# Moving operands of TensorE placed 64 bytes beyond their stationary ones, modulo 256 bytes, in a three-stage attention and MLP kernel

## Chip, cores, metric

The kernel runs on one core of a Trainium2 chip. The metric is the device time of one execution in microseconds (us); lower is better. TensorE (PE), VectorE (DVE), ScalarE (ACT), GpSimd (POOL) and SyncE (SP) each run their own instruction stream; weight loads of TensorE are shown apart as PEld.

## The reference

Batch 2, sequence 3136, model width 256. Three layers follow each other:

```python
scores = z @ z.T / 3136                       # d_qk = 64
x = u * (maximum(scores, 0)**2 @ v)           # attention, gated

h = x.T @ U @ V                               # rank 32, over the sequence
a = x + h.T
x = a + maximum(a @ w_ch1, 0) @ w_ch2         # layer 1, hidden width 1024

m = real(fft(fft(x, axis=1), axis=2))
a = x + m
un = (a - mean(a)) / sqrt(var(a) + 1e-6)
out = a + maximum(un @ w_ch1b, 0) @ w_ch2b    # layer 2
```

## The kernel before

All matrix products are in fp32r (fp32 data read by TensorE in one pass). To keep precision, each operand is split into a high and a low part, and each product is three matmuls: high x high, high x low, low x high. Nearly every matmul has a moving operand of 448 columns (`CH`).

**Attention** (`attention`, from L421). For each batch and each of 7 blocks of 448 queries there are 13 steps, one a pair of key blocks. `scores` (L574) writes a key block's scores to PSUM: K = 64 (the head width), so two matmuls share the array, one on partitions 0 to 63 and one on 64 to 127; stationary is `KT`, moving is `Q`. ACT and DVE turn the scores into `P`, `h` (high) and `l` (low). `products` (L616) multiplies them by the values, two steps later (`LAG`): stationary is `Vt`, moving are `h` and `l`, again 64 rows in each half of the array. A full step has 3 pairs of matmuls for scores and 12 for values, so 15 pairs; a block of 13 steps has 186 pairs, 3 of them only 224 columns wide.

**Layers 1 and 2** (`Chunk`, L246). A layer has 14 chunks of 448 tokens, and a chunk 8 steps. A step issues 12 full 128-row matmuls: six in `hidden` (L368, L369, L370, twice: stationary the first weight matrix, moving `h` and `l`), then six in `project` for an earlier step (L393, L394, L395, twice: stationary the second weight matrix, moving `Hh` and `Hl`, the split result of `hidden`). Between the steps stand a few matmuls of other work: low-rank sums (L234), the Fourier transform (L956 to L958, L995, L1013 to L1018), layer norm sums (L308, L327).

The order of the instructions is written out by hand (`tc.manual_schedule()`), and tiles come from pools in which they lie one behind the other, so a tile's byte address in a partition follows from the sizes of the tiles and pools declared before it. The pools in question are `const` (masks, Fourier tables, the low-rank table `Us`, the low-rank factors `Gs`), `com` (`P`, `h`, `l`, `Vs`), `wpool` (8 weight tiles), `att` and `big` (attention: `zraw`, `qraw`, `Q`, `KTl`, `uT`, `KT`, `Vt`), and, in the place of the last two after attention, `mp` (among others `Hh`, `Hl`, `Th`, `Tl`, `nh`, `nl`, `alt`) and `wpool2` (4 weight tiles: the first weight matrix of layer 2). Every operand of a matmul starts a multiple of 256 bytes into its tile (parts of 512 or 1,024 bytes of a stationary tile; 448 columns of 4 bytes are 7 x 256), so its place modulo 256 is that of its tile. As the built program places them (bytes modulo 256):

| stage, lines | stationary | moving | moving beyond stationary |
|---|---|---|---|
| attention scores, L574 | `KT`, `KTl`: 0 | `Q`: 0 | 0 |
| attention values, L616 | `Vt`: 0 | `h`, `l`: 0 | 0 |
| layer 1 hidden, L368 to L370 | `w` of `wpool`: 0 | `h`, `l`: 0 | 0 |
| layer 1 project, L393 to L395 | `w` of `wpool`: 0 | `Hh`, `Hl`: 64 | 64 |
| layer 2 hidden, L368 to L370 | `w` of `wpool2`: 192 | `h`, `l`: 0 | 64 |
| layer 2 project, L393 to L395 | `w` of `wpool`: 0 | `Hh`, `Hl`: 64 | 64 |
| Fourier, L956 to L958, L1013 to L1018 | tables: 0 | `nh`, `nl`, `Th`, `Tl`: 64 | 64 |

(The scores of the single narrow step of a block, 224 columns wide, have 0 and 128 in the last column.) So the attention and layer 1's hidden matmuls have both operands at the same place modulo 256 bytes, and the rest of layers 1 and 2 already has the 64 bytes.

`alternating` (L926) is a small DVE step of the Fourier work: it writes a difference to the scratch tile `alt` and sums it into `top`, 16 times in all.

Of the kernel before, what the change touches and what calls it, by code (L numbers as in the profile page):

```python
# [10 lines left out]
F32 = mybir.dt.float32  # L11
F32R = mybir.dt.float32r
# [9 lines left out]
CH = 448  # L22
# [52 lines left out]
def f(ap):  # L75
    return ap.bitcast(F32)
# [3 lines left out]
def program(ctx, tc, zT, v, uT, U, V, w1a, w2a, w1b, w2b, b49, f64, fd, rep, mask, out):  # L80
# [8 lines left out]
    def hcopy(o, i):  # L89
        nc.scalar.copy(o, i)  # L90

    def sub(o, a, b):
        tt(out=o, in0=a, in1=b, op=ALU.subtract)  # L93

    const = ctx.enter_context(tc.tile_pool(name="const", bufs=1))
    com = ctx.enter_context(tc.tile_pool(name="com", bufs=3))
# [25 lines left out]

    ident = const.tile([128, 128], F32, name="ident")
    repc = const.tile([128, 128], F32, name="repc")
    maskc = const.tile([128, 32], F32, name="maskc")
    b49h = const.tile([128, 128], F32R, name="b49h")
    b49l = const.tile([128, 128], F32R, name="b49l")
    f64s = const.tile([128, 128], F32, name="f64s")
# [2 lines left out]
    ones = const.tile([128, 128], F32R, name="ones")  # L131
    Us = const.tile([128, 26, RANK], F32, name="Us")
    Gs = [const.tile([128, D], F32R, name=f"Gs{b}") for b in range(NB)]

    def constants(t):
        make_identity(nc, ident)
        late_dma(out=repc, in_=rep)
        late_dma(out=maskc[:, 0:7], in_=mask)
        late_dma(out=t[0:98, 0:128], in_=b49)
        late_dma(out=f64s, in_=f64)  # L140
        late_dma(out=t[:, 256:512], in_=fd)
        nc.vector.memset(t[:, 768:896], 1.0 / D)
        for _ in range(3):
            yield
        hcopy(ones, t[:, 768:896])
        for x in (b49h, b49l):
            nc.gpsimd.memset(f(x), 0.0)
        hcopy(b49h[0:98], t[0:98, 0:128])
        sub(b49l[0:98], t[0:98, 0:128], f(b49h[0:98]))
        yield  # L150
        for dst, k in ((fA, 256), (fB, 384)):
            hcopy(dst[:, 0], t[:, k : k + 128])
            sub(dst[:, 1], t[:, k : k + 128], f(dst[:, 0]))
            if dst is fA:
                yield
# [23 lines left out]
    def fetch_w(raw, src, k, second):  # L179
        if second:  # L180
            load(out=raw[:, 0:512], in_=src[k * 128 : k * 128 + 128, :])
        else:
            load(
                out=raw[:, 0:512].rearrange("p (a n) -> p a n", a=2),
                in_=src[:, k * 256 : k * 256 + 256].rearrange("(a p) n -> p a n", p=128),
            )
# [33 lines left out]
    def misc():  # L220
        p, tag = misc_pools[misc_at[0] % len(misc_pools)]
        misc_at[0] += 1
        return p.tile([128, 512], F32, tag=tag, name="ps_" + tag)
# [23 lines left out]
    class Chunk:  # L247
# [2 lines left out]
            self.sl = slice(c * CH, c * CH + CH)  # L250

        def load(self):
            self.vs = com.tile([128, CH], F32R, tag="Vs", name="Vs", bufs=1)
            for k in (0, 64):
                late_dma(out=self.vs[k : k + 64, :], in_=V_d[:, self.sl])

# [166 lines left out]
    def attention(stack):  # L423
        att = stack.enter_context(tc.tile_pool(name="att", bufs=2))
# [8 lines left out]
        zraw, qraw, vraw = {}, {}, {}  # L433
# [14 lines left out]
        def split_z(b, i):  # L448
            raw = zraw.pop((b, i))
            if i == 0:  # L450
                KT[b] = big.tile([128, 12, 2, 128], F32R, tag="KT", name=f"KT_{b}")
            if i < 4:
                dst = KT[b][:, 3 * i : 3 * i + 3]
                hcopy(dst[:, :, 0], raw)
                sub(dst[:, :, 1], raw, f(dst[:, :, 0]))
                return
            t = KTl[b] = att.tile([128, 2, 128], F32R, tag="KTl", name="KTl")
            for c in (0, 64):
                hcopy(t[:, 0, c : c + 64], raw[:, 0, 0:64])
                sub(t[:, 1, c : c + 64], raw[:, 0, 0:64], f(t[:, 0, c : c + 64]))  # L460

        def load_q(b, qc):
            t = qraw[b, qc] = att.tile([128, CH], F32, tag="qraw", name="qraw", bufs=1)
            for r in halves[0 : 1 if (b, qc) == (0, 0) else 2]:
                (late_dma if (b, qc) == (0, 1) else load)(out=t[r], in_=zT[b, :, qc * CH : qc * CH + CH])

# [266 lines left out]
        t = att.tile([128, 5, D], F32R, tag="an", name="warm", bufs=1).rearrange("p a n -> p (a n)")  # L733
# [7 lines left out]
        for k in range(32):  # L741
            r, n = halves[k % 2], 128 if k < 8 else 352
# [3 lines left out]
        load_v(0, 2)  # L746
        split_q(0, 0)
        split_z(0, 0)
        split_v(0, 0)
        scores(0, 0, 0)  # L750

        def ahead(i):
            if i < len(steps):
# [28 lines left out]
                if b == 0 and qc == 5 and p < 6:  # L782
                    if p < 5:
                        load_z(1, p)
                    if p > 0:
                        split_z(1, p - 1)

        for i in range(-LAG, len(steps)):
# [3 lines left out]
            if i >= 0:  # L792
                b, qc, p = steps[i]
# [6 lines left out]
                n = i % NP  # L800
# [6 lines left out]
                if (b, qc) == (1, NC - 1):  # L807
                    if p == 2:
                        chunks[0].load()
                        a = att.tile([128, 2, CH], F32, tag="uT", name="uT")  # L810
# [21 lines left out]
    mp = late["mp"] = ctx.enter_context(tc.tile_pool(name="mp", bufs=2))  # L832
# [12 lines left out]
    rows = [mp.tile([128, CH], F32, tag=f"row{k}", name=f"row{k}", bufs=1) for k in range(2)]  # L845
    late["half"] = rows[0][:, 0:D]
    y = mp.tile([128, 416], F32, tag="y", name="y", bufs=1)
    top = [mp.tile([98, 32], F32, tag=f"top{b}", name=f"top{b}", bufs=1) for b in range(NB)]
    for t in (raw128, col128, y[:, 392:416]):
        nc.gpsimd.memset(t, 0.0)  # L850
# [8 lines left out]
    def pair_late():  # L859
        nats.append(nats.pop(0))  # L860
        return nats[-1]
# [33 lines left out]
    def halves49(b):  # L895

        nat = {}
        x0, x1 = (xT[b][:, a].rearrange("p (s m r) -> p s m r", m=49, r=2) for a in range(2))
        yv = y[:, 0:392].rearrange("p (s m r) -> p s m r", m=49, r=2)

        def fold(i):

            s0, s1 = 4 * i, 4 * i + 4
            for t0, t1 in ((0, 1), (1, s1)) if s0 == 0 else ((s0, s1),):
                for m, w in ((0, 0), (1, 25), (25, 1)):
                    n = 24 if m else 1
                    in1 = x1[:, t0:t1, w : w + n]
                    if t0:
                        in1 = in1[:, :, :, ::-1]
                    tt(  # L910
                        out=yv[:, t0 - s0 : t1 - s0, m : m + n],
                        in0=x0[:, t0:t1, m : m + n],
                        in1=in1,
                        op=ALU.add,
                    )
            yt = mp.tile([128, 416], F32, tag="A1" if i == 7 else "yt", name="yt", bufs=1)
            nc.vector.transpose(out=yt, in_=y)
            for c in (0, 32, 64, 96):
                (load if c < 64 else late_dma)(
                    out=nat_d[b][i, :, c : c + 32].rearrange("(j t) d -> t j d", t=32),  # L920
                    in_=yt[c : c + 32].rearrange("p (j d) -> p j d", d=32),
                )
            if i == 7:
                load(out=raw128[0:32, 0:98], in_=xT[b][0:1, 1, :].rearrange("o (s p) -> o s p", p=98))

        def alternating(i, x):  # L926

            v = x[0:98].rearrange("p (s d r) -> p s d r", s=4, r=2)
            t = mp.tile([98, 4, 64], F32, tag="alt", name="alt", bufs=1)
            sub(t, v[:, :, :, 0], v[:, :, :, 1])  # L930
            nc.vector.reduce_sum(out=top[b][0:98, 4 * i : 4 * i + 4], in_=t, axis=mybir.AxisListType.X)

        def fetch(i):
            h, l = nat[i] = pair_late()
            load(
                out=f(l)[0:98].rearrange("p (s d) -> p s d", s=4),
                in_=nat_d[b][i, 0:392].rearrange("(s p) d -> p s d", p=98),
            )

        def tokens(i):  # L940
            h, l = nat[i]
            hcopy(h[0:98], f(l)[0:98])
            alternating(i, f(l))
            sub(l[0:98], f(l)[0:98], f(h[0:98]))

        def axis49(i):
            ps = misc()
            dft49(ps, *nat.pop(i))
            w = mp.tile([128, 512], F32, tag="wst", name="wst")
            hcopy(w, ps)  # L950
            load(out=scr[b][:, 4 * i : 4 * i + 4, :], in_=w.rearrange("p (s d) -> p s d", s=4))

        return fold, fetch, tokens, axis49

    def dft49(ps, h, l):
        mm(ps, b49h, h, start=True, stop=False)  # L956
        mm(ps, b49h, l, start=False, stop=False)  # L957
        mm(ps, b49l, h, start=False, stop=True)  # L958

    def fourier(b):  # L960
# [40 lines left out]

        def feature128():
            ps = misc()
            e = mp.tile([57, 64], F32, tag="ech", name="ech", bufs=1)
            mm(ps[:, 0:64], col128, f64s[:, 0:64], start=True, stop=True)
            hcopy(e, ps[0:57, 0:64])
            late_dma(out=e_d[b].rearrange("(p n) -> p n", n=64), in_=e)
# [118 lines left out]
    with tc.manual_schedule():  # L1126
# [21 lines left out]
        for i in range(nstep + 2):  # L1148
# [23 lines left out]
            if i in fetches:  # L1172
                b, k0, k1 = fetches[i]
# [57 lines left out]
```

## Time and profile before

| | |
|---|---|
| time, median of 3 runs | 1132.77 us (1132.64 to 1133.49) |
| time of the profiled execution | 1132.07 us |
| its span, first to last instruction | 1130.3 us |
| PE busy, share of the span | 1125.1 us, 100% |
| PEld busy | 1061.7 us, 94% |
| DVE, ACT, POOL busy | 847.0, 633.7, 181.5 us |
| granted TensorE clock over the span | 1.000 |
| matmuls | 8310 |

The span starts with the first instruction and ends with the last, so 1.8 us of the profiled execution lie around it. Matmuls overlap each other in the pipeline, so a busy share of 100% says that PE is never without one in flight, and not how closely they follow each other: that is read from the starts of successive matmuls in the timeline.

### The profile page before, as it was taken

To read this page: it belongs to the slowest core of one execution; us is meant where nothing else is said; L and a number is where in the kernel's file an instruction comes from. 1 tells how busy PE (TensorE), PEld (TensorE's weight loads), DVE (VectorE), ACT (ScalarE), POOL (GpSimd) and SP (SyncE) were. 2 spreads that over 40 slices of the span, in tenths; PEclk is the share of its full clock that TensorE was granted. 3 is DMA by queue.
4 is the path that set the end of the run, shared out by engine and by line. 5 is a ranking of instruction groups with operands and counts; after the bars stand their busy time and mean duration, and the time that the engine had idled before them with its cause. 6 is when DMAs were issued, how large, how long until landed. Compare 5 with 4: busy or idle time off the path is not lost.

```text
span 1130.3 us, 21424 instructions
## 1 busy us (share of the span) xinstructions
PE 1125.1 (100%) x8310; PEld 1061.7 (94%) x8310; DVE 847.0 (75%) x1571; ACT 633.7 (56%) x1032; POOL 181.5 (16%) x299
## 2 busy tenths in 40 slices
PE   9999999999999999999999999999999999999998
PEld 8999999999999999999989999999999999999997
DVE  8877888888887667676667777577588888777863
ACT  8777777878786666675334444343345444444431
POOL 2202310221022102202221112111131100000010
PEclk9999999999999999999999999999999999999999
DMA  5212322324123302111823455231143321111111
GB/s 168 75 46 61 104 80 69 119 71 127 47 72 118 121 18 59 50 36 32 265 62 95 128 159 130 74 75 45 47 107 100 76 48 42 33 42 33 42 33 42
DMA packets 86758, 88.96 MB, mean 79 GB/s; under 512 B 27398, under 2 KB 76034, under 8 KB 86656
## 3 DMA queue, kind: packets, MB, share of 16 engines
q1 hardware_dynamic: 70272, 58.44, 17.2%
q0 software_dynamic: 16032, 28.93, 10.2%
q8 instruction: 65, 1.06, 0.4%
q14 instruction: 37, 0.30, 0.1%
q10 hardware_dynamic: 352, 0.21, 0.1%
HBM read 57.67 MB, written 29.82 MB: 77 GB/s over the span
## 4 chain that ended last, share of the span: by engine, by line
PE 99%; ACT 0%; DVE 0%; issue 0%; DVEq 0%; POOL 0%; POOLq 0%
PE psO L616 37%; PE psS L574 9%; PE psH L368 8%; PE psH L369 8%; PE psC L394 8%; PE psC L395 8%; PE psH L370 8%; PE psC L393 8%; PE psS L743 0%; PE ps_m L995 0%; PE ps_g L995 0%; PE ps_x L995 0%; PE psS L234 0%; PE ps_g L234 0%; PE ps_m L958 0%; PE ps_m L957 0%
## 5 line engine op out<-in xcount | busy, mean ns | idle before, releaser
L616 PE MATMUL psO<-h,Vt 64*128 64x448 f32 x2744 | 345.1, 363 | 0.2 <-DVE h L585 0.2
L616 PEld LDWEIGHTS psO<-h,Vt 64*128 64x128 f32 x2744 | 294.4, 185 | 9.1 <-DVE h L585 0.7
L93 DVE TENSOR_TENSOR l<-P,h 128x896 fp32r<-128x896 f32 (+2 forms) x237 | 224.8, 954 | 33.3 <-ACT h L90 16.4
L373 ACT ACTIVATE Hh<-psH 128x448 fp32r<-128x448 f32 x224 | 121.0, 541 | 201.5 <-PE psH L370 198.3
L374 DVE SCALAR_TENSOR_TENSOR Hl<-psH,Hh 128x448 fp32r<-128x448 f32 x224 | 138.3, 620 | 117.9 <-ACT Hh L373 115.7
L590 ACT ACTIVATE P<-psS 128x896 f32<-128x896 f32 (+1 forms) x181 | 160.2, 885 | 85.4 <-PE psS L574 84.6
L616 PE MATMUL psO<-l,Vt 64*128 64x448 f32 x1372 | 206.4, 363 | 0.0
L592 DVE CAST h<-P 128x896 fp32r<-128x896 f32 (+1 forms) x181 | 110.9, 613 | 85.0 <-ACT P L591 83.8
L591 ACT ACTIVATE P<-P 128x896 f32<-128x896 f32 (+1 forms) x181 | 167.4, 925 | 5.7
L368 PE MATMUL psH<-h,w 128*128 128x448 f32 x448 | 166.5, 372 | 0.0
L616 PEld LDWEIGHTS psO<-l,Vt 64*128 64x128 f32 x1372 | 159.9, 185 | 4.4 <-DVE l L93 0.3
L369 PE MATMUL psH<-l,w 128*128 128x448 f32 x448 | 163.4, 365 | 0.0
L394 PE MATMUL psC<-Hl,w 128*128 128x448 f32 x448 | 163.4, 365 | 0.0
L370 PE MATMUL psH<-h,w 128*128 128x448 f32 x448 | 162.9, 364 | 0.0
L393 PE MATMUL psC<-Hh,w 128*128 128x448 f32 x448 | 162.9, 364 | 0.0
L395 PE MATMUL psC<-Hh,w 128*128 128x448 f32 x448 | 162.7, 363 | 0.0
L574 PE MATMUL psS<-Q,KT 64*128 64x448 f32 x1002 | 147.6, 364 | 0.0
L574 PEld LDWEIGHTS psS<-Q,KT 64*128 64x128 f32 x1002 | 115.2, 185 | 3.7 <-issue 0.4
L368 PEld LDWEIGHTS psH<-h,w 128*128 128x128 f32 x448 | 84.3, 188 | 7.9 <-issue 0.3
L393 PEld LDWEIGHTS psC<-Hh,w 128*128 128x128 f32 x448 | 84.2, 188 | 6.8 <-issue 0.2
L370 PEld LDWEIGHTS psH<-h,w 128*128 128x128 f32 x448 | 84.2, 188 | 6.5
L394 PEld LDWEIGHTS psC<-Hl,w 128*128 128x128 f32 x448 | 84.2, 188 | 6.3 <-DVE Hl L374 0.5
(313 smaller groups left out, 1157.1 us busy)
## 6 DMA issues: line engine op xcount, KB each, us to landing
out<-P SPq DMA_DIRECT2D x27, 224.0 KB, 1.9
uT<-in_uT SPq DMA_DIRECT2D x13, 448.0 KB, 4.0
aTd<-aT POOLq DMA_DIRECT2D x13, 448.0 KB, 3.1
aNd<-aT POOLq DMA_DIRECT2D x104, 56.0 KB, 2.4
vraw<-in_v SPq DMA_DIRECT2D x18, 256.0 KB, 2.7
scr<-wst SPq DMA_DIRECT2D x16, 256.0 KB, 2.0
Vs<-Vd POOLq DMA_DIRECT2D x28, 112.0 KB, 2.6
xT<-aTd SPq DMA_DIRECT2D x7, 448.0 KB, 4.6
```

Source lines behind the costliest of these rows:

```text
L93: tt(out=o, in0=a, in1=b, op=ALU.subtract)
L368: mm(ps[:, 0:CH], wh, self.h[:, a], start=a == 0, stop=False)
L369: mm(ps[:, 0:CH], wh, self.l[:, a], start=False, stop=False)
L370: mm(ps[:, 0:CH], wl, self.h[:, a], start=False, stop=a == 1)
L374: stt(out=l, in0=ps[:, 0:CH], scalar=0.0, in1=f(h), op0=ALU.max, op1=ALU.subtract)
L393: mm(dst, wh, h, start=k == 0, stop=False)
L394: mm(dst, wh, l, start=False, stop=False)
L395: mm(dst, wl, h, start=False, stop=k == 7)
L574: mm(dst[:, 0:w], k, q[r, kq, o : o + w], start=(kk, kq) == (0, 0), stop=kk == 1)
L590: act(out=A[:, x].rearrange("p (a n) -> p a n", a=2), in_=ps[:, :, 0:w], func=AF.Relu, scale=1.0 / S)
L591: act(out=A[:, x], in_=A[:, x], func=AF.Square)
L616: mm(o[fa][i][:, 0:CH], vt[r, j, k, fa * 128 : fa * 128 + 128], x[r, j * CH : j * CH + CH], start=p == 0 and fa not in [t[1][0] for t in t ...
```

## The change

Tiles get spare columns so that addresses shift, and one scratch tile moves. `maskc` loses 64 bytes and a tile `gap` of 64 bytes is put behind `Gs`, so the tables between them (with `Gs` and `Us`) start 64 bytes lower, and `com` stays where it was. `Vs` gets 192 bytes more, which moves `wpool` and all behind it. In `att`, `qraw` gets 64 bytes and a `gap` of 192 bytes is put before `KTl`. `alt` is gone from `mp`; its place is taken by the first 256 columns of `Us`. `ech` gets 64 bytes. The spare columns are never read or written: all instructions keep their sizes.

```diff
-    maskc = const.tile([128, 32], F32, name="maskc")
+    maskc = const.tile([128, 16], F32, name="maskc")
...
     Gs = [const.tile([128, D], F32R, name=f"Gs{b}") for b in range(NB)]
+    const.tile([128, 16], F32, name="gap")
...
         def load(self):
-            self.vs = com.tile([128, CH], F32R, tag="Vs", name="Vs", bufs=1)
+            self.vs = com.tile([128, CH + 48], F32R, tag="Vs", name="Vs", bufs=1)[:, 0:CH]
...
+            if b == 0:
+                att.tile([128, 48], F32, tag="gap", name="gap", bufs=1)
             t = KTl[b] = att.tile([128, 2, 128], F32R, tag="KTl", name="KTl")
...
         def load_q(b, qc):
-            t = qraw[b, qc] = att.tile([128, CH], F32, tag="qraw", name="qraw", bufs=1)
+            t = qraw[b, qc] = att.tile([128, CH + 16], F32, tag="qraw", name="qraw", bufs=1)[:, 0:CH]
...
+    spare = Us.rearrange("p a n -> p (a n)")
...
         def alternating(i, x):
...
-            t = mp.tile([98, 4, 64], F32, tag="alt", name="alt", bufs=1)
+            t = spare[0:98, 0:256].rearrange("p (s d) -> p s d", s=4)
             sub(t, v[:, :, :, 0], v[:, :, :, 1])
...
-            e = mp.tile([57, 64], F32, tag="ech", name="ech", bufs=1)
+            e = mp.tile([57, 80], F32, tag="ech", name="ech", bufs=1)[:, 0:64]
```

As the built program places them now (bytes modulo 256): `KT`, `KTl`, `Vt`, all weight tiles, `Gs` and the tables at 192; `Q`, `h`, `l`, `Hh`, `Hl`, `nh`, `nl`, `Th`, `Tl` and `Vs` at 0. So every fp32r matmul of the program has its moving operand 64 bytes beyond the stationary one modulo 256, but for the warm-up, the first six scores (which take both operands from `Q`), half of the narrow scores (192), and one matmul of each layer norm line (L308, L327: 192). Sizes, engines, the order on every engine and its queues, and the waits are the same before and after. The one place where an instruction reads differently is `alternating`. On DVE, at its first use in the program (`Hl` is the split in `hidden`, `nl` the transform's low part, `top` the sums), before:

```order
L374 SCALAR_TENSOR_TENSOR Hl<-psH,Hh 128x448 [waits Activation_49]
L93 TENSOR_TENSOR alt<-nl_7826 98x256 [waits DMAHW1_49,Pool_49]
L931 TENSOR_REDUCE top_7820<-alt 98x4 [waits DVE_49]
L93 TENSOR_TENSOR nl_7826<-nl_7826,nh_7825 98x512 [waits Activation_49]
L93 TENSOR_TENSOR Tl<-Tl 128x256
```

and now:

```order
L375 SCALAR_TENSOR_TENSOR Hl<-psH,Hh 128x448 [waits Activation_49]
L93 TENSOR_TENSOR Us<-nl_7828 98x256 [waits DMAHW1_49,Pool_49]
L935 TENSOR_REDUCE top_7822<-Us 98x4 [waits DVE_49]
L93 TENSOR_TENSOR nl_7828<-nl_7828,nh_7827 98x512 [waits Activation_49]
L93 TENSOR_TENSOR Tl<-Tl 128x256
```

The subtraction writes to `Us`, and it waits for what it waited for before.

## Rows read from the trace of the kernel before

**Rows 1.** The page: busy time by engine, and the chain that ended last.
```profile
PE 1125.1 (100%) x8310; PEld 1061.7 (94%) x8310; DVE 847.0 (75%) x1571; ACT 633.7 (56%) x1032; POOL 181.5 (16%) x299
...
PE 99%; ACT 0%; DVE 0%; issue 0%; DVEq 0%; POOL 0%; POOLq 0%
```

**Rows 2.** The page's groups: line, engine, operation, tiles, shapes, count, busy us, mean ns.
```profile
L616 PE MATMUL psO<-h,Vt 64*128 64x448 f32 x2744 | 345.1, 363 | 0.2 <-DVE h L585 0.2
...
L616 PE MATMUL psO<-l,Vt 64*128 64x448 f32 x1372 | 206.4, 363 | 0.0
L368 PE MATMUL psH<-h,w 128*128 128x448 f32 x448 | 166.5, 372 | 0.0
...
L574 PE MATMUL psS<-Q,KT 64*128 64x448 f32 x1002 | 147.6, 364 | 0.0
```

**Rows 3.** Busy time by stage: attention, layer 1, layer 2 (instruction counts in brackets).
```profile
core 0: us, PE busy (x) PEld busy (x) DVE busy (x) ACT busy (x) POOL busy (x), PEclk, DMA share, GB/s
5.00:537.00 532.00, 531.78 (x5277) 512.79 (x5274) 417.34 (x632) 390.26 (x527) 94.11 (x144) 1.00 0.26 77
537.00:835.00 298.00, 298.00 (x1536) 274.69 (x1536) 204.97 (x454) 119.66 (x249) 52.17 (x89) 1.00 0.39 107
835.00:1127.00 292.00, 291.32 (x1474) 270.23 (x1472) 222.94 (x485) 121.74 (x254) 34.76 (x61) 1.00 0.20 52
```

**Rows 4.** PE's timeline in layer 1: six steps, first and last matmul's starts.
```profile
612.43 0.36 PE L368 MATMUL psH<-h,w 128*128 128x448 f32 x1
...
626.99 0.36 PE L368 MATMUL psH<-h,w 128*128 128x448 f32 x1
```

**Rows 5.** PE's timeline in layer 2: four and a half steps; 13 steps.
```profile
978.64 0.36 PE L368 MATMUL psH<-h,w 128*128 128x448 f32 x1
...
989.49 0.36 PE L368 MATMUL psH<-h,w 128*128 128x448 f32 x1
...
1089.97 0.36 PE L368 MATMUL psH<-h,w 128*128 128x448 f32 x1
...
1121.34 0.37 PE L368 MATMUL psH<-h,w 128*128 128x448 f32 x1
```

**Rows 6.** Busy time in stretches of layer 1 (first three) and layer 2.
```profile
549.50:564.06 14.56, 14.56 (x73) 13.52 (x72) 9.28 (x21) 6.04 (x13) 1.08 (x2) 1.00 0.82 248
612.42:626.98 14.56, 14.56 (x73) 13.53 (x72) 11.10 (x27) 5.59 (x13) 2.47 (x4) 1.00 0.42 112
789.35:803.91 14.56, 14.56 (x73) 13.52 (x72) 10.45 (x23) 5.38 (x10) 2.44 (x4) 1.00 0.21 45
978.63:989.48 10.85, 10.85 (x55) 10.14 (x54) 8.41 (x19) 4.75 (x10) 1.11 (x2) 1.00 0.12 21
1057.96:1068.81 10.85, 10.85 (x55) 10.13 (x54) 8.17 (x20) 4.78 (x10) 1.10 (x2) 1.00 0.12 21
```

**Rows 7.** PE's timeline in the attention, two successive steps of 15 pairs.
```profile
259.72 1.61 PE L616 MATMUL psO<-h,Vt 64*128 64x448 f32 x14
...
262.76 1.61 PE L616 MATMUL psO<-h,Vt 64*128 64x448 f32 x14
```

**Rows 8.** The same earlier: each half of the array at the same place of three steps.
```profile
182.75 0.36 PE L616 MATMUL psO<-l,Vt 64*128 64x448 f32 x1
182.79 0.36 PE L616 MATMUL psO<-h,Vt 64*128 64x448 f32 x1
...
185.79 0.36 PE L616 MATMUL psO<-l,Vt 64*128 64x448 f32 x1
185.89 0.36 PE L616 MATMUL psO<-h,Vt 64*128 64x448 f32 x1
...
188.83 0.36 PE L616 MATMUL psO<-l,Vt 64*128 64x448 f32 x1
188.99 0.37 PE L616 MATMUL psO<-h,Vt 64*128 64x448 f32 x1
```

**Rows 9.** The chain that ended last: the same piece of successive attention blocks.
```profile
115.39 5.06 PE psO L616 x41
153.00 4.87 PE psO L616 x48
...
265.99 4.66 PE psO L616 x46
303.41 4.66 PE psO L616 x46
```

**Rows 10.** The scratch tile's instructions (ns min/median/max, first and last start).
```profile
L93 DVE TENSOR_TENSOR alt<-nl x16: 404/416/427, 636.2 to 854.9; 98x256 f32<-98x256 f32 x16
L931 DVE TENSOR_REDUCE top<-alt x16: 419/420/423, 636.6 to 855.3; 98x4 f32<-98x256 f32 x16
```

**Rows 11.** The last matmuls that read the low-rank table.
```profile
L234 PE MATMUL ps_g<-xT,Us x48: 378/379/403, 569.4 to 571.8; 128*32 128x256 f32 x48
```

## The prediction

> **What bounds the kernel now.** I read the page first: one matmul or another is in flight for 100% of the span, and the chain of work that ended last runs through PE for 99% [rows 1]. No other engine holds it up for a share that matters, so the time is the number of matmuls times the distance between their starts. The groups give the numbers [rows 2]: in the attention 2,744 + 1,372 matmuls on values and 1,002 on scores, which run as pairs, one in each half of the array, so (4,116 + 1,002) / 2 = 2,559 pairs of 448 columns. L368 stands for six lines with 448 matmuls each, half in each layer; a layer is 14 chunks x 8 steps x 12 = 1,344 matmuls. The mean of 363 to 372 ns in these rows is how long one matmul is in flight, nearly two starts, and says nothing of the rate. By stage, the attention takes 532 us, layer 1 298 and layer 2 292 [rows 3], at a granted clock of 1.00, the 2.4 GHz level. There 448 columns need 448 / 2.4 = 186.7 ns.
>
> The distance between starts is read from the timeline, over a stretch that holds nothing but 448-column matmuls. Layer 1: from 612.43 to 626.99 us there are six steps, 72 matmuls: 14.56 / 72 = 202.2 ns each [rows 4]. Layer 2: 54 matmuls in 10.85 us are 200.9 ns, 156 in 31.37 us are 201.1 [rows 5]; I use 201.0. Attention: successive steps of 15 pairs start 3.04 us apart, 202.7 ns a pair [rows 7]. So each matmul costs 14 to 16 ns more than its columns.
>
> Now the comparison on which everything rests. Layer 1 and layer 2 issue the same twelve matmuls a step, with the same `h`, `l`, `Hh`, `Hl`, the same pool for the second weights and the same PSUM tiles. What differs in the operands is one thing: the first weight matrix lies at 0 modulo 256 bytes in layer 1 and at 192 in layer 2, so that six of twelve matmuls have their moving operand 0 bytes, or 64, beyond the stationary one. The other six have 64 in both layers. Does the load of the other engines or of the DMAs explain the 1.2 ns instead? Three stretches of layer 1 take 14.56 us each while the DMA share falls from 0.82 to 0.21 and DVE is busy for 9.28 to 11.10 us; two of layer 2 take 10.85 each with DVE at 8.41 and 8.17 [rows 6]. (73 and 55 count the matmul still running at the start.) A rate that repeats to the hundredth of a microsecond under such different loads comes from the instructions themselves, and their addresses are what differs.
>
> **The change part by part.** No instruction is added, dropped or reordered, and no wait changes. What may change is how closely matmuls follow each other.
>
> Layer 1: its six matmuls at distance 0 move to 64, so that every step has what a step of layer 2 has now. 1,344 x (202.2 - 201.0) = 1.6 us less.
>
> Layer 2: already at 64 throughout; nothing.
>
> Attention: all pairs move from 0 to 64. No row shows a 64-row pair at 64. Bounds: nothing, if pairs in half arrays are held by something else than full matmuls are; or, at the other end, the whole step's saving in layer 1 put on its six changed matmuls, 12 x 1.2 / 6 = 2.4 ns a pair, 6.1 us. Below nothing stands as a rival. I take the value that the nearest row gives: the pairs at 0 go at 202.7, much like a step of layer 1 with its half at 0, and at 64 I let them go at layer 2's 201.0. That is 1.7 x 2,559 = 4.3 us less.
>
> A part of the attention goes slower still. From 182.75 to 188.99 us the first half of the array keeps 3.04 us a step (182.75, 185.79, 188.83) while the second takes 3.10 (182.79, 185.89, 188.99), 206.7 ns [rows 8]: the halves drift apart and the later one sets the pace. A block with such a stretch takes 37.61 us (115.39 to 153.00) against 37.42 (265.99 to 303.41) [rows 9]. I leave these stretches as they are; if they went, that would be some tenths of a microsecond for each block that has one.
>
> The scratch tile: 16 subtractions of 416 ns and 16 sums of 420 on DVE, now through `Us` [rows 10]. The sizes are the same. The hazard would be a wait for the last read of `Us`, and that ended at 572 us while the first use is at 636 [rows 11]: 64 us of cover; without it the DVE step would wait for PE, with the splits of `hidden` behind it. Cost 0.
>
> Spare columns and shifted addresses for ACT, DVE and the DMAs: 0. In the attention, the busiest stage, DVE is at 417 of 532 us and ACT at 390 [rows 3]; PE running 1% faster brings neither to its limit.
>
> The sum against the profiled execution: 1132.07 - 1.6 - 4.3 = 1126.2 us. The median of the runs shown stands 0.7 us above that execution, so the forecast on the median is 1132.77 - 5.9 = **1126.9 us**. With 1.0 to 2.4 ns a pair in the attention the likeliest case covers 1125.1 to 1128.6.
>
> **Rivals.** *Addresses don't matter* (chance 0.06). What rows 6 show is a rate that follows the layer, and layers differ in more than the first weights' place: other weight values, another pool. Then nothing changes: 1132.8 us. Against it stands that each layer's rate is the same in every stretch.
> The Trainium skill speaks for this rival. Its page "TensorE: Matmul & The Clock Gate" (Part 2, on what each phase is for) gives PE two independent read ports into SBUF, one for the streaming operand and one for the weights; by that, where the two lie relative to each other could cost nothing, and the sum would hold no term. The 1.2 ns between the layers [rows 4, 5] speak against taking it so strictly.
>
> *Half arrays don't gain* (0.13). The two halves of a pair load and stream in separate partitions, and the paces of rows 7 and 8 could be set by how the halves alternate. Then only layer 1's 1.6 us come: 1131.2 us, within 0.2% of before. For it: no row shows such a pair at 64. Against it: at 0 the pair's 202.7 ns is close to the full matmul's rate, as if the same thing held both.
>
> *Pairs fall into the slow pace* (0.08), the one on the other side. The 206.7 ns of rows 8 belong to a half that has come to lie late behind the other. If 64 bytes let the halves fall apart more easily, all pairs could go so: (206.7 - 202.7) x 2,559 = 10.2 us more, less 1.6, so 1141.4 us. It is slower than before once over 0.41 of the pairs are in that pace: with a share f, -1.6 - 4.3 (1 - f) + 10.2 f passes zero there. For it: the pace exists in the profile. Against it: it holds a small part of the attention, where both operands are at the same place.
>
> *The change doesn't place what it says*: excluded by the table of places above.
>
> **How the numbers follow.** The forecast has a chance of 0.73 (1125.1 to 1128.6, with some room to either side), half arrays without gain 0.13, addresses without effect 0.06, slow pace 0.08. The range goes from 1124.5, which is the upper bound of the attention's gain and half a microsecond of slow stretches gone, to 1131.5, which takes in the case with layer 1 alone; it leaves out 0.06 + 0.08 and little more. About 0.2%, 2.3 us, is what a measurement of this kernel can tell from no change: faster by more than that is the forecast's 0.73; the two middle cases give 0.19 for the same; the slow pace 0.08.
>
> **What would show it.** In the profile after: a layer 1 stretch of 72 matmuls should take 14.47 us in place of 14.56, and 54 of layer 2 stay at 10.85. A step of 15 pairs should take 3.015 us in place of 3.04, and an undisturbed attention block 37.42 - 183 x 0.0017 = 37.11. Busy times and counts of DVE and ACT stay. The forecast is wrong in its attention term if blocks stay at 37.42, wrong altogether if layer 1 also stays at 202.2, and the slow pace has won if steps of 3.10 stand in most blocks.

## The result and the profile after

| | before | after |
|---|---|---|
| time, median of 4 runs each | 1132.73 us (1132.64 to 1133.49) | 1120.65 us (1120.50 to 1120.88) |
| profiled execution, span | 1132.07, 1130.3 us | 1120.5, 1118.7 us |
| attention, to the first L368 / L369 of layer 1 | 536.73 us | 528.93 us |
| layer 1, to the first one of layer 2 | 298.32 us | 295.87 us |
| layer 2, to the start of the last matmul | 290.90 us | 289.58 us |

The ratio of after to before is 0.9892, 95% interval 0.9875 to 0.9909: 12.1 us faster. The forecast was 5.9 us, and the range ended at 1124.5: the sign was right, the size was not. By stage the profiled executions differ by 7.8 us in the attention, 2.45 in layer 1 and 1.3 in layer 2.

The page after, busy time, chain and groups (counts as in [rows 1, 2], lines three further down):

```profile
PE 1113.3 (100%) x8310; PEld 1054.1 (94%) x8310; DVE 845.9 (76%) x1571; ACT 633.6 (57%) x1032; POOL 181.0 (16%) x299
...
PE 98%; ACT 1%; DVE 1%; issue 0%; DVEq 0%; POOL 0%; ACTq 0%; POOLq 0%
...
L619 PE MATMUL psO<-h,Vt 64*128 64x448 f32 x2744 | 324.7, 359 | 0.2 <-DVE h L588 0.2
...
L619 PE MATMUL psO<-l,Vt 64*128 64x448 f32 x1372 | 186.3, 359 | 0.1
...
L369 PE MATMUL psH<-h,w 128*128 128x448 f32 x448 | 165.4, 369 | 0.0
...
L577 PE MATMUL psS<-Q,KT 64*128 64x448 f32 x1002 | 132.7, 360 | 0.0
```

Every count is the same, and DVE and ACT are busy for what they were within 1.1 us. PE still bounds the kernel, and nearly all of the 11.6 us by which the span is shorter lies in how closely its matmuls follow each other. That is read from PE's timeline after (start us, duration us, engine, line): six steps of layer 1, then 54 matmuls of layer 2, then four steps of it.

```profile
799.90 0.36 PE L369 MATMUL psH<-h,w 128*128 128x448 f32 x1
...
814.30 0.36 PE L369 MATMUL psH<-h,w 128*128 128x448 f32 x1
...
967.89 0.36 PE L369 MATMUL psH<-h,w 128*128 128x448 f32 x1
...
978.69 0.36 PE L369 MATMUL psH<-h,w 128*128 128x448 f32 x1
...
1100.18 0.36 PE L369 MATMUL psH<-h,w 128*128 128x448 f32 x1
...
1109.78 0.36 PE L369 MATMUL psH<-h,w 128*128 128x448 f32 x1
```

Layer 1: 72 matmuls in 14.40 us. Layer 2: 54 in 10.80 and 48 in 9.60. All three are 200.0 ns a matmul, where [rows 4, 5] had 202.2 and 201.0. A step of twelve is 2.400 us in both layers; before it was 2.4265 in layer 1 (14.56 / 6) and 2.413 in layer 2. So layer 2 became faster too, and the forecast had left it alone.

Two of these stretches by windows, after (columns as in [rows 3]):

```profile
799.89:814.28 14.39, 14.39 (x73) 13.49 (x72) 9.91 (x21) 5.04 (x9) 3.46 (x6) 1.00 0.27 65
1100.18:1109.77 9.59, 9.59 (x49) 8.99 (x48) 2.48 (x5) 2.18 (x4) 0.00 (x0) 1.00 0.00 1
```

The pace is the same with DVE busy for 69% of the stretch as with 26%, and with a DMA share of 0.27 as with none; the granted clock is 1.00 in both, the 2.4 GHz level.

The attention's chain of waits after, four blocks that follow each other, and below it its timeline in the block that held the drifted halves of [rows 8] (x16: eight matmuls of either half):

```profile
224.94 4.81 PE psO L619 x48
...
261.91 4.80 PE psO L619 x48
...
298.86 4.81 PE psO L619 x48
...
335.82 4.81 PE psO L619 x48
```

```profile
178.81 1.76 PE L619 MATMUL psO<-h,Vt 64*128 64x448 f32 x16
...
181.81 1.76 PE L619 MATMUL psO<-h,Vt 64*128 64x448 f32 x16
```

A block takes 36.95 to 36.97 us where an undisturbed one took 37.42 [rows 9]; a step of 15 pairs takes 3.00 us, again 200.0 ns a pair, and here both halves keep it. No stretch of steps of 3.10 us is left in the chain. The third block still takes 37.41 us, and that is no slow stretch but a wait of PE's weight loads for DVE, which was there before too; before and after:

```profile
117.34 0.30 PEld L616 LDWEIGHTS psO<-l,Vt 64*128 64x128 f32 x4 [0.30 <-DVE l L93]
...
115.73 0.30 PEld L619 LDWEIGHTS psO<-l,Vt 64*128 64x128 f32 x4 [0.49 <-DVE l L93]
```

The scratch tile, DVE's lines after against [rows 10, 11]:

```profile
L93 DVE TENSOR_TENSOR Us<-nl x16: 402/414/426, 627.6 to 844.6; 98x256 f32<-98x256 f32 x16
L935 DVE TENSOR_REDUCE top<-Us x16: 419/420/422, 628.1 to 845.0; 98x4 f32<-98x256 f32 x16
```

16 subtractions of 414 ns and 16 sums of 420, as before: it costs nothing.

### The profile page after: what moved, and what is told of

The parts are those of the page before. It is cut to its first block, busy times and chain, and to the rows that moved or that the text cites. A ratio compares the mean times of both kernels' runs of the same rounds, so it can differ in the third digit from the quotient of the medians.

```text
span 1118.7 us, 21424 instructions
## 1 busy us (share of the span) xinstructions
PE 1113.3 (100%) x8310; PEld 1054.1 (94%) x8310; DVE 845.9 (76%) x1571; ACT 633.6 (57%) x1032; POOL 181.0 (16%) x299
## 4 chain that ended last, share of the span: by engine, by line
PE 98%; ACT 1%; DVE 1%; issue 0%; DVEq 0%; POOL 0%; ACTq 0%; POOLq 0%
PE psO L619 36%; PE psS L577 9%; PE psC L394 8%; PE psC L395 8%; PE psC L396 8%; PE psH L369 8%; PE psH L371 8%; PE psH L370 8%; PE psS L746 0%; PE ps_m L999 0%; PE ps_g L999 0%; PE ps_x L999 0%; PE psS L235 0%; PE ps_g L235 0%; DVE l L93 0%; PE ps_m L961 0%
## 5 line engine op out<-in xcount | busy, mean ns | idle before, releaser
L619 PE MATMUL psO<-h,Vt 64*128 64x448 f32 x2744 | 324.7, 359 | 0.2 <-DVE h L588 0.2
L619 PEld LDWEIGHTS psO<-h,Vt 64*128 64x128 f32 x2744 | 277.4, 184 | 8.2 <-DVE h L588 0.7
L619 PE MATMUL psO<-l,Vt 64*128 64x448 f32 x1372 | 186.3, 359 | 0.1
L369 PE MATMUL psH<-h,w 128*128 128x448 f32 x448 | 165.4, 369 | 0.0
L395 PE MATMUL psC<-Hl,w 128*128 128x448 f32 x448 | 162.1, 362 | 0.1
L370 PE MATMUL psH<-l,w 128*128 128x448 f32 x448 | 162.0, 362 | 0.0
L619 PEld LDWEIGHTS psO<-l,Vt 64*128 64x128 f32 x1372 | 144.1, 184 | 4.4 <-DVE l L93 0.7
L577 PE MATMUL psS<-Q,KT 64*128 64x448 f32 x1002 | 132.7, 360 | 0.0
L577 PEld LDWEIGHTS psS<-Q,KT 64*128 64x128 f32 x1002 | 103.2, 184 | 3.5 <-issue 0.4
L369 PEld LDWEIGHTS psH<-h,w 128*128 128x128 f32 x448 | 84.2, 188 | 7.0 <-ACT P L90 0.3
L395 PEld LDWEIGHTS psC<-Hl,w 128*128 128x128 f32 x448 | 83.9, 187 | 6.3 <-DVE Hl L375 0.7
```

Of the source, the lines that this page charges most:

```text
L369: mm(ps[:, 0:CH], wh, self.h[:, a], start=a == 0, stop=False)
L370: mm(ps[:, 0:CH], wh, self.l[:, a], start=False, stop=False)
L395: mm(dst, wh, l, start=False, stop=False)
L577: mm(dst[:, 0:w], k, q[r, kq, o : o + w], start=(kk, kq) == (0, 0), stop=kk == 1)
L619: mm(o[fa][i][:, 0:CH], vt[r, j, k, fa * 128 : fa * 128 + 128], x[r, j * CH : j * CH + CH], start=p == 0 and fa not in [t[1][0] for t in t ...
```

## The experiments

Each kernel was timed once beside one run of the kernel before on the same chip. All do the same work with the same instructions in the same order, apart from how weight tiles and their loads are cut in one of them; what differs is where tiles lie. The steadier readings are a step of twelve matmuls in a layer (112 in each) and an undisturbed attention block (14 in all). Diffs are against the kernel after unless said.

**First: absolute place, no distance, and one stage alone.** In the first kernel `maskc` keeps its 128 bytes, so that everything behind lies 64 bytes higher: stationary operands at 0, moving ones at 64. In the second the tables, weights and moving tiles all lie at 0.

```diff
-    maskc = const.tile([128, 16], F32, name="maskc")
+    maskc = const.tile([128, 32], F32, name="maskc")
```

> All stationary operands at 0 and all moving ones at 64 modulo 256 bytes: the distance of the change, at another absolute place. Theory 'next load' (a matmul's moving stream is slowed by the weight load for the following matmul, and only the distance between those two operands counts): steps of 12 matmuls at 2.400 us in both layers, attention blocks near 36.95 us, time 1120.6 us as with the change. Rival 'absolute place' (weights at 192, or moving operands at 0, are what is fast): no better than before, 1132 us or more. Rival 'own pair' (the distance to a matmul's own weights counts, and layer 2 of the kernel before showed the rate at 64): steps at 2.413 us, time about 1123.

The second has this edit and the widths of the row "0" in the table further down.

> Both operands at 0 modulo 256 bytes everywhere, also in the twelve matmuls of both layers. 'Next load': each stream over a load at distance 0 costs (2.4265 - 2.400) / 6 = 4.4 ns, now 12 of them a step: steps at 2.453 us in both layers, attention block as before at 37.42 us, time 1132.8 + 112 x 0.0265 + 112 x 0.0395 = 1140.2 us. 'Own pair': 2.2 ns for each of six more matmuls in layer 1 and twelve in layer 2, steps at 2.440 us, time 1137.3. 'Absolute place': the weights of the hidden matmuls at 0 as in layer 1 before, steps at 2.426 us, about 1134.

The third is the kernel before with one tile added in the attention; the fourth is the kernel after without that tile.

```diff
+            if b == 0:
+                att.tile([128, 48], F32, tag="gap", name="gap", bufs=1)
```

> The kernel before with one tile of 192 bytes ahead of KTl: the attention's pairs at distance 64, both layers as they were. All theories: the attention's share of the gain alone. By the traces 7.8 us of the 12.1: blocks at 36.95 us, steps at 2.426 us (layer 1) and 2.413 us (layer 2), time 1124.9 us. If the gain of the attention were due to something else in the change (the loads of wpool, Us as scratch): nearer to 1132.

> The change without its part in the attention: keys and values at 0 modulo 256 bytes, both layers at distance 64 for own weights and for the following ones. 'Next load': steps at 2.400 us in both layers, 112 x 0.0265 + 112 x 0.0135 = 4.5 us less than before, blocks at 37.42 us, time 1128.3 us. 'Own pair': layer 2 stays at 2.413 us, layer 1 comes to 2.413 too, time 1131.2.

| | time, us | before beside it | step, layer 1 / 2, us | block, us |
|---|---|---|---|---|
| before | 1132.73 | | 2.4265 / 2.413 | 37.42 |
| after | 1120.65 | 1132.73 | 2.400 / 2.400 | 36.95 |
| moving 64, stationary 0 | 1121.40 | 1132.84 | 2.400 / 2.400 | 36.95 |
| all at 0 | 1137.95 | 1132.84 | 2.43 or 2.48 in both | 37.42 |
| attention alone | 1124.64 | 1132.84 | 2.4265 / 2.413 | 36.95 |
| layers alone | 1129.10 | 1132.84 | 2.400 / 2.400 | 37.42 |

PE's timeline with all at 0: six steps of layer 1 and four of layer 2.

```profile
593.30 0.37 PE L368 MATMUL psH<-h,w 128*128 128x448 f32 x1
...
608.18 0.37 PE L368 MATMUL psH<-h,w 128*128 128x448 f32 x1
...
1117.43 0.36 PE L368 MATMUL psH<-h,w 128*128 128x448 f32 x1
...
1127.15 0.37 PE L368 MATMUL psH<-h,w 128*128 128x448 f32 x1
```

72 matmuls in 14.88 us are 206.7 ns, 48 in 9.72 are 202.5: at distance 0 the full-array matmuls of the layers have the two paces that the attention had before [rows 7, 8]. None of the three theories named beforehand had two paces in it. PE's timeline with moving at 64 and stationary at 0, the same places in the program:

```profile
800.80 0.36 PE L369 MATMUL psH<-h,w 128*128 128x448 f32 x1
...
815.20 0.36 PE L369 MATMUL psH<-h,w 128*128 128x448 f32 x1
...
1101.08 0.36 PE L369 MATMUL psH<-h,w 128*128 128x448 f32 x1
...
1110.68 0.36 PE L369 MATMUL psH<-h,w 128*128 128x448 f32 x1
```

14.40 and 9.60 us, the kernel after to the hundredth. So it isn't the absolute place that counts, and 16.6 us (1137.95 against 1121.40) lie between two kernels with the same instructions whose operands differ by 64 bytes. That settles the rival by which addresses don't matter. The Trainium skill's two independent read ports, which spoke for it (the page "TensorE: Matmul & The Clock Gate", Part 2, on what each phase is for), do not make the pace independent of where the two operands lie: the measurement decides.

With the attention alone changed, its chain reads:

```profile
225.19 4.81 PE psO L618 x48
...
262.15 4.80 PE psO L618 x48
...
299.11 4.81 PE psO L618 x48
```

Blocks of 36.96 us and 8.2 us in all: half arrays gain, and that rival falls too. With the layers alone changed, PE's timeline in layer 2:

```profile
1108.75 0.36 PE L369 MATMUL psH<-h,w 128*128 128x448 f32 x1
...
1118.35 0.36 PE L369 MATMUL psH<-h,w 128*128 128x448 f32 x1
```

Four steps in 9.60 us, where before they took 9.65 (1111.69 to 1121.34). The two parts add: 8.2 + 3.7 = 11.9 us of the 11.4 to 12.1 that both give together. By the steps the layers alone should have given 4.5 us; their attention, at distance 0 as before, took 0.8 us longer than before (537.53 us against 536.73), with more slow stretches. The last reading is the puzzle that the remaining runs are about: before, every matmul of layer 2's steps already had its moving operand 64 bytes beyond its own weights, and the change left that distance as it was. What it moved was the place of the operands: in layer 2 before, `hidden` had 0 and 192, `project` 64 and 0; now both have 0 and 192.

**Second: other distances.** Is 64 special, or is anything but 0 as good? One series sets the distance everywhere, by the widths in the table (in columns of 4 bytes; `gap2` is a tile added in `mp` ahead of `raw128`).

| distance | `maskc` | `gap` in `const` | `Vs` + | `gap` in `att` | `qraw` + | `gap2` | `ech` |
|---|---|---|---|---|---|---|---|
| 64 (after) | 16 | 16 | 48 | 48 | 16 | none | 80 |
| 0 | 32 | none | 0 | none | 0 | 48 | 96 |
| 32 | 24 | 8 | 56 | 56 | 8 | 56 | 88 |
| 96 | 8 | 24 | 40 | 40 | 24 | 8 | 72 |
| 128 | 64 | 32 | 32 | 32 | 32 | 16 | 64 |
| 192 | 48 | 48 | 16 | 16 | 48 | 32 | 112 |
| 224 | 40 | 56 | 8 | 8 | 56 | 40 | 104 |

> Moving operands 128 bytes beyond the stationary ones everywhere (moving at 0, stationary at 128). Theory 'coincidence' (only operands at the same place modulo 256 bytes collide; any other distance is free): steps of 12 at 2.400 us, blocks at 36.95 us, time 1120.7 us. Rival 'each distance has its price' (layer 2 of the kernel before lost 13 ns a step on one load at 0 and one at 128; with 2.7 ns for the one at 0, as in the run with all at 0, some 10 ns are left for the one at 128): steps up to 2.400 + 12 x 0.010 = 2.52 us, blocks above 37.42 us, slower than before.

> Moving operands at 0, stationary at 64: 192 bytes beyond, or 64 short of. 'Coincidence': steps at 2.400 us, blocks 36.95 us, time 1120.7 us. Rival 'the moving operand has to be ahead' (the order of the two matters, since the stream runs faster than the load and overtakes it): steps and blocks above that, at 2.432 us and 37.42 us or more, time 1132 or more.

> Moving operands 32 bytes beyond. 'Coincidence': as at 64, 2.400 us and 36.95 us, time 1120.7 us. If the width of the collision is 64 bytes or more: part of the loss at 0 comes back, steps between 2.400 and 2.432 us, time between 1120.7 and 1138.

> Moving operands 96 bytes beyond. 'Coincidence': 2.400 us and 36.95 us, time 1120.7 us. If each distance has its price, a value between those at 64 and at 128; if it lies under 2.400 us, 64 bytes are not the best distance.

> Moving operands 224 bytes beyond (32 short of) the stationary ones everywhere. If odd multiples of 32 bytes are the slow ones, as 32 and 96 were: steps near 2.46 us and blocks near 37.9 us, time about 1146 us. If only what lies just ahead of the load collides: as at 192 or faster, steps at 2.427 us or less, 1131.6 us or less.

Two more move only the attention's stationary tiles, by 16 bytes up or down, so that its distance is 48 or 80. The edit for 48 (for 80 the `gap` in `att` is 40 columns instead of 48 as well):

```diff
-                KT[b] = big.tile([128, 12, 2, 128], F32R, tag="KT", name=f"KT_{b}")
+                KT[b] = big.tile([128, 3136], F32R, tag="KT", name=f"KT_{b}")[:, 4:3076].rearrange("p (a h n) -> p a h n", a=12, h=2)
...
-            t = KTl[b] = att.tile([128, 2, 128], F32R, tag="KTl", name="KTl")
+            t = KTl[b] = att.tile([128, 320], F32R, tag="KTl", name="KTl")[:, 4:260].rearrange("p (a n) -> p a n", a=2)
...
-            t = Vt[b, p] = big.tile([128, 2, 2, D], F32R, tag="V", name="Vt", bufs=13)
+            t = Vt[b, p] = big.tile([128, 1088], F32R, tag="V", name="Vt", bufs=13)[:, 4:1028].rearrange("p (a h n) -> p a h n", a=2, h=2)
```

> The change with keys and values 16 bytes higher: the attention's moving operands 48 bytes beyond, the layers at 64. If the free distance is a range around 64: blocks at 36.95 us, time 1120.7 us. If 64 is a single good place between 32 (pairs at 204 to 207 ns) and 96 (205): blocks between 37.0 and 37.9 us, time 1121 to 1134 us. A block under 36.95 would be a better place than the change's.

> The same with keys and values 16 bytes lower: 80 bytes beyond in the attention, 64 in the layers. Range around 64: blocks at 36.95 us, time 1120.7 us. Single good place: blocks between 37.0 and 37.9 us, time 1121 to 1134 us. Under 36.95: a better place.

| distance | time, us | before beside it | ns a matmul in the layers | block, us |
|---|---|---|---|---|
| 0 | 1137.95 | 1132.84 | 202.5 or 206.7 | 37.42 |
| 32 | 1145.21 | 1134.50 | 204.4 or 206.7 | 37.5 to 37.9 |
| 48, attention only | 1131.28 | 1132.49 | 200.0 (at 64) | 37.73 to 37.75 |
| 64 (after) | 1120.65 | 1132.73 | 200.0 | 36.95 |
| 80, attention only | 1131.53 | 1132.49 | 200.0 (at 64) | 37.54 to 37.86 |
| 96 | 1147.18 | 1134.50 | 205.4 | 37.91 |
| 128 | 1140.02 | 1134.50 | 203.3 to 204.6 | 37.66 |
| 192 | 1131.59 | 1134.50 | 202.2 | 37.34 |
| 224 | 1141.27 | 1132.49 | 203.3 or 204.4 | 37.65 to 37.75 |

PE's timeline at distance 96, four steps of layer 2 (9.86 us, 205.4 ns):

```profile
1126.48 0.37 PE L369 MATMUL psH<-h,w 128*128 128x448 f32 x1
...
1136.34 0.36 PE L369 MATMUL psH<-h,w 128*128 128x448 f32 x1
```

and the chain with the attention at 48, one block (37.74 us):

```profile
229.51 4.91 PE psO L619 x48
...
267.25 4.91 PE psO L619 x48
```

Of the nine places tried, 64 alone reaches 200.0 ns, and it is no broad valley: 16 bytes to either side cost 0.6 to 0.9 us a block, so that the attention is slower than at distance 0, and 32 bytes to either side are the two slowest kernels of all. Each against the before beside it, 96 is 12.7 us slower and 64 is 12.1 us faster: some 25 us lie between them. That any distance but 0 is free, the first theory here, is wrong, and no other that was named beforehand gives these values: 32 and 96 were expected between their neighbours and came out slower than both, and 224 came out between its two theories.

**Third: whose weights count?** While one matmul streams, the next one's weights are loaded: before, L370's load starts at 799.87 us and takes 0.19, while L369's matmul, started at 799.87 as well, takes 0.36. Layer 2's gain at an unchanged distance to its own weights could mean that the distance to the next matmul's weights is what counts: in layer 2 before, that one was off 64 wherever `hidden` and `project` met. The ninth kernel tells the two apart: high weights at 192, low weights at 0, high moving operands at 0, low ones at 64. Then a matmul's own weights are 64, 128 or 0 away, and those of the matmul that follows 64 throughout.

```diff
+        if tag == "l" and "l" not in placed:
+            com.tile([128, 16], F32, tag="gl", name="gl", bufs=1)
...
+    def wtiles(pool):
+        wh = pool.tile([128, 2, 256], F32R, tag="wh", name="wh")
+        if id(pool) not in placed:
+            pool.tile([128, 16], F32, tag="gw", name="gw", bufs=1)
+        wl = pool.tile([128, 2, 256], F32R, tag="wl", name="wl")
...
-                self.t[part] = self.pool.tile([128, 2, 2, 256], F32R, tag="w", name="w")
+                self.t[part] = wtiles(self.pool)
...
+            if "Hl" not in placed:
+                mp.tile([128, 16], F32, tag="gH", name="gH", bufs=1)
```

> In both layers the high weights lie at 192, the low ones at 0, the high moving parts at 0 and the low ones at 64. A matmul's distance to its own weights is now 64, 128, 0 for the three of a product; its distance to the weights that are loaded for the following matmul while it streams is 64 for all, also from hidden to project and back. 'Next load': steps stay at 2.400 us in both layers. 'Own pair': 4 x (200.0 + 204.1 + 202.7) = 2.427 us a step, by the rates of the runs with one distance everywhere. In the attention the low part streams at 128 by both theories, some 50 of 186 pairs at 4 ns more: blocks near 37.15 us. Time 1123.5 us by 'next load', 1129.5 by 'own pair'.

The time was 1136.34 us beside 1132.49. PE's timeline, six steps of layer 1 and four of layer 2:

```profile
809.25 0.37 PE L387 MATMUL psH<-h,wh 128*128 128x448 f32 x1
...
824.13 0.37 PE L387 MATMUL psH<-h,wh 128*128 128x448 f32 x1
...
1115.55 0.37 PE L387 MATMUL psH<-h,wh 128*128 128x448 f32 x1
...
1125.26 0.37 PE L387 MATMUL psH<-h,wh 128*128 128x448 f32 x1
```

2.480 and 2.427 us a step, as slow as at distance 0: 64 to the next weights alone gives nothing in the layers. The prices of each matmul's own distance add up to 2.427, which some stretches of layer 2 take; the 2.480 of the others no theory named beforehand gave. In the attention of this kernel the prices do add up: only `l` lies at another distance there, 128, and a block takes 37.18 us, where 49 pairs at 4 ns more give 37.15. Two last kernels look at places. In one, every matmul of layer 2 keeps 64 to its own weights, but `hidden` has moving 0 and weights 192, and `project` 128 and 64 (layer 1's `hidden` then has 192). In the other only `Hl` moves, by 128 bytes, so that 2 of 12 matmuls have 192.

```diff
-    maskc = const.tile([128, 16], F32, name="maskc")
+    maskc = const.tile([128, 48], F32, name="maskc")
...
-    const.tile([128, 16], F32, name="gap")
+    const.tile([128, 48], F32, name="gap")
...
-            self.vs = com.tile([128, CH + 48], F32R, tag="Vs", name="Vs", bufs=1)[:, 0:CH]
+            self.vs = com.tile([128, CH + 16], F32R, tag="Vs", name="Vs", bufs=1)[:, 0:CH]
...
-            t = qraw[b, qc] = att.tile([128, CH + 16], F32, tag="qraw", name="qraw", bufs=1)[:, 0:CH]
+            t = qraw[b, qc] = att.tile([128, CH + 48], F32, tag="qraw", name="qraw", bufs=1)[:, 0:CH]
...
-            e = mp.tile([57, 80], F32, tag="ech", name="ech", bufs=1)[:, 0:64]
+            e = mp.tile([57, 112], F32, tag="ech", name="ech", bufs=1)[:, 0:64]
```

> Layer 2 with every matmul 64 bytes beyond its own weights, but hidden and project in two places: hidden moving at 0 on weights at 192, project moving at 128 on weights at 64; across the two borders of a step the distance to the following weights is 192. (Layer 1's hidden matmuls are 192 beyond theirs; attention as with the change.) 'Own pair': layer 2's steps at 2.400 us. 'Next load': two of twelve loads at 192, which cost 2.2 ns a matmul in the run with 192 everywhere, so 2.404. 'One place each' (the flat rate needs all moving operands in one place and all stationary ones in another, so each switch of places costs beyond that): 2.413 us or more, as in the kernel before, whose borders were at 0 and 128.

```diff
+            first = not hasattr(Chunk, "placed")
+            if first:
+                mp.tile([128, 32], F32, tag="gH", name="gH", bufs=1)
...
+            if first:
+                mp.tile([128, 32], F32, tag="gH2", name="gH2", bufs=1)
+                Chunk.placed = True
```

> The change with Hl alone 128 bytes further: in project the two low matmuls of six are 192 bytes beyond their weights, all else at 64 in both layers. If each matmul pays by its distance, to its own weights or to the following ones alike: 2 x 2.2 = 4.4 ns a step, 2.404 us, time 1121.2 us. 'One place each': more, 2.413 us or above in both layers, time 1122 us or above.

The times were 1124.41 and 1124.25 us beside 1132.80. PE's timeline with two places, four steps of layer 2:

```profile
1104.06 0.37 PE L369 MATMUL psH<-h,w 128*128 128x448 f32 x1
...
1113.69 0.37 PE L369 MATMUL psH<-h,w 128*128 128x448 f32 x1
```

and with `Hl` moved, six steps of layer 1 and four of layer 2:

```profile
801.83 0.37 PE L369 MATMUL psH<-h,w 128*128 128x448 f32 x1
...
816.39 0.37 PE L369 MATMUL psH<-h,w 128*128 128x448 f32 x1
...
1103.86 0.36 PE L369 MATMUL psH<-h,w 128*128 128x448 f32 x1
...
1113.51 0.36 PE L369 MATMUL psH<-h,w 128*128 128x448 f32 x1
```

With two places most steps of layer 2 take 2.407 us, though every matmul has 64 to its own weights: the own distance alone doesn't explain it either. Only the first step of a stretch, behind other work, takes 2.400 to 2.403. None of the three theories gave that: 2.400 by the own distance, 2.404 by the next, 2.413 or more if all operands of a kind must lie in one place. With `Hl` moved a step takes 2.413 to 2.427, as the last of the three had it here too, or 2.405 as the first of a stretch: if each matmul had a price by its own distance, two at the 202.2 ns of distance 192 would give 10 x 200.0 + 2 x 202.2 = 2.404. Two matmuls out of place cost three to six times that 0.004 in most steps, so others around them are slowed as well. The starts in layer 2 show it: `hidden`'s six matmuls, all in place, take 1,202 ns together in a step of 2.413 us and 1,203 in one of 2.427, where they take 1,200 with the change; `project`'s six take 1,211 and 1,223. What the kernels with a flat 2.400 in both layers share (after, moving 64, layers alone, and the two with the attention at 48 and 80) is that all moving operands of the layers lie in one place, all weights in one other, 64 bytes apart. No run that departs from this keeps 2.400 beyond the first step of a stretch, but no theory named beforehand gives the size of the loss; which read meets which in TensorE or in the memory the runs don't show, and it stays open. No kernel tried beats the change.

## Why the prediction was right in sign and short in size

- **What bounds the kernel, and that addresses set the pace.** Right. The comparison of layer 1 with layer 2 found the cause from 1.2 ns, though both rates were those of mixed places, and moving operands by 64 bytes against their weights moves the time by 16.6 us from the worst of the two kernels to the best.
- **"Layer 2: already at 64 throughout; nothing."** This is the step that failed. Layer 2 had 64 from each operand to its own weights but sat in two places, and its 201.0 ns was the pace of that mixture. With one place it runs at 200.0: a step goes from 2.413 to 2.400, 112 x 0.0135 = 1.5 us, of which 1.3 came.
- **Layer 1, 1.6 us.** Right mechanism, end point wrong by the same step: not 201.0 but 200.0, so 112 x 0.0265 = 3.0 us by the step. The stage became 2.45 us shorter. Of the 0.5 us that are missing, 0.2 are one weight load (L395), which waits 0.43 us for `Hl` where it waited 0.25; the rest was not followed.
- **Attention, 4.3 us.** "At 64 I let them go at layer 2's 201.0" took over the same mixture. A pair goes from 202.7 to 200.0: 2.7 ns, beyond the upper bound of 2.4 that the prediction had worked out by putting the step's saving on the six changed matmuls. Clean blocks give 14 x 0.465 = 6.5 us of the measured 7.8.
- **The slow stretches "left as they are".** They went, and of the 1.3 us that are left of the attention's 7.8 that is some 1.1. Another 0.5 is luck: the first values matmul started at 8.00 us instead of 8.54, and over the sixteen profiles that start lies anywhere from 7.65 to 8.82. Against both stand 0.3 us of the third block, which became 0.20 us shorter where a clean one gained 0.47. This is the block that the prediction gave as one with a slow stretch (115.39 to 153.00, 37.61 us [rows 9]): what it held was the wait for `l`. The block with the stretch of [rows 8] is the next, and took 37.80 us. The rival by which pairs fall into the slow pace did not come at 64.
- **Scratch tile, DVE, ACT, DMAs at 0.** Right: durations and busy times stayed. Only the wait for `l` in the third block of the attention grew with the faster PE, from 0.30 to 0.49 us.

With 200.0 in place of 201.0 the prediction's own sum reads 1,344 x 2.2 = 3.0, 1,344 x 1.0 = 1.3 and 2,559 x 2.7 = 6.9, together 11.2 us against 12.1 measured. One wrong rate, used three times, is nearly the whole error. It could have been doubted from the rows at hand: the table of places showed that layer 2 used two pairs of places, and 202.2 with half of the matmuls at 0 against 202.7 with all of them at 0 was a poor fit to a price per matmul that ends at 201.0 [rows 4, 5, 7].

## What to carry to other kernels

Where TensorE is never idle and the time is set by the distance between starts, work out the addresses of its moving and stationary operands modulo 256 bytes, and put all of each kind in one place, at a distance that is measured: for the fp32r matmuls of 448 columns here, 64 bytes were worth 12.1 us, and 96 cost 12.7. Whether 64 is the good distance for other widths or types no run shows. Read the rate from start to start over a stretch, not from busy shares or mean durations, and don't take the rate of a program that mixes places for the rate of one of them. When a tile is added or resized in a tuned kernel, look again at what it shifted behind it.

## What was not expected of the hardware

- The pace often settles on a grid. Step times of 2.400, 2.413, 2.427, 2.440, 2.453 and 2.480 us, which come again and again, lie a multiple of about 13.3 ns apart. Others lie off it: 2.407 with two places, 2.432 at distance 0, 2.445 at 128.
- One program runs at two paces in stretches. At distance 0 a step of the layers takes 2.43 us in one stretch and 2.48 in another, with the same instructions; at 32 it is 2.453 or 2.480. The kernel before showed that only for halves of the array, and the prediction put it down to the halves drifting apart; full-array matmuls do it too. What tips a stretch into the one or the other wasn't found.
- The dependence is fine and not monotonic: of the distances tried everywhere, 192 (202.2 ns) is the best after 64, and 32 and 96 are worse than 0 in time.
